# Last rows of w1 as 128 half rows on the main queue, hidden units numbered by halves, w1 issued first, small vectors on the second queue

## The chip, the cores and the metric

The kernel runs on one core of a Trainium2 chip. The core has five engines with instruction streams of their own: TensorE (PE, with its weight loads shown as PEld), VectorE (DVE), ScalarE (ACT), GpSimd (POOL) and SyncE (SP). SP and ACT also issue transfers between the chip's memory and the core's 128-partition memory; in the profile their issuing rows are SPq and ACTq, and their two queues are q1 and q10. The metric is the device time of one execution in microseconds, lower is better. The profile gives one execution in detail.

## The reference

Two branches of one decoder step are mixed by a gate. Eight tokens (B = 8), width D = 448.

```python
def _A_ref(x, k_cache, v_cache, wq, wo):      # 16 heads of 256 over 8 K/V heads, window W = 1024
    q = (x @ wq).reshape(B, Sq, Hq, Dh).transpose(0, 2, 1, 3)
    k = jnp.repeat(k_cache[:, :, Sk - W:, :], rep, axis=1)
    v = jnp.repeat(v_cache[:, :, Sk - W:, :], rep, axis=1)
    p = softmax(jnp.einsum("bhqd,bhkd->bhqk", q, k) * (Dh ** -0.5))
    o = jnp.einsum("bhqk,bhkd->bhqd", p, v)
    return o.transpose(0, 2, 1, 3).reshape(B, Sq, Hq * Dh) @ wo

def _B_ref(x, w1, b1, w2, b2):                # 448 -> 1792 -> 448
    h = gelu(jnp.einsum("bsd,df->bsf", layernorm(x), w1) + b1)
    return jnp.einsum("bsf,fd->bsd", h, w2) + b2

g = sigmoid((x * gate_w).sum(-1, keepdims=True))
return g * _A_ref(...) + (1 - g) * _B_ref(x, ...)
```

All inputs and the output are bfloat16. In bytes the K and V windows are nearly all: 64 pairs of token and K/V head, with one K tile and one V tile of 512 KB each.

## The kernel before

**Loads.** Nearly all transfers are issued by SP, in a fixed order: x (L121), the first 384 rows of w1 (L125), w2 (L130), three pieces of wq (L134) and wq's last 64 rows as 128 half rows (L135), then K tiles, V tiles and slices of wo in the order of the list `units`. ACT issues the gate vector (L122), the last 64 rows of w1 (L128) into partitions 0 to 63 of `w1_t`, b1 into partition 64 of the same tile (L129) and b2 (L131). K and V tiles share a ring of 23 buffers (NKV). A new tile is issued when the tile that had its buffer has been read, and each issue also waits for the transfer eight places earlier in the order of all issues of both queues; the order is written out by hand.

A row of w1 is one of D input features, a column one of F = 1792 hidden units. The first 384 features lie three to a partition in `w1_sb`. The last 64 features lie one to a partition in `w1_t`, with b1 below them as a 65th row; the transposed input `yT` has a row of ones there (the memset at L173).

**Start.** VectorE forms the gate's sum and the layer norm of x (L179 to L198), with a square root and a tanh on ScalarE. `transposed` (L207) turns y (three thirds and the last 64 columns) and x (three thirds and two spread halves `x_e`) into columns with TensorE and copies them out of PSUM.

**Feed-forward.** `mlp_up` (L231) works on 14 groups of 128 hidden units; unit q * 14 + k is unit q of group k. A group is four matmuls into eight columns of one PSUM tile: three for `w1_sb`, one of 65 partitions for `w1_t` and the bias. The gelu follows on VectorE and ScalarE, and `mlp_down` (L258) multiplies group by group with `w2_sb`, which holds 14 consecutive rows of w2 on each partition, in one run of 12544 bytes.

**Queries and attention.** Then q is formed from wq (L280 to L299), and the main loop (L432) runs over 64 pairs: `transposes` of a K tile, `scores` of the pair before, the softmax once per K/V head, and `pv` with the V tile of the pair eleven places back. `issue_to(NKV + done)` at the end of each step issues the next tiles on SP. After the loop comes the last projection and the gated sum (L458).

Of the kernel before, what the change touches and what calls it, by code (L numbers as in the profile page):

```python
# [11 lines left out]
BF16 = mybir.dt.bfloat16  # L12
# [4 lines left out]
def kernel(  # L17
# [15 lines left out]
    nc = tc.nc  # L33
    P = nc.NUM_PARTITIONS

    B, Sq, D = A_x.shape
# [4 lines left out]
    W = min(4096, max(256, Sk // 4))  # L41
    kv0 = Sk - W
    F = B_w1.shape[1]
    NB = B
    NJ = Dh // P
    NC = W // P
    NF = F // P
    R = NB * rep
    DC = D // P
    DM = DC * P  # L50
    TL = D - DM
    HH = HD // 2
    assert Sq == 1 and Dh % P == 0 and W % P == 0 and F % P == 0
    assert TL * 2 == P and TL % 32 == 0 and NC * R <= P and 3 * 32 <= P and R <= 32
    qscale = float(Dh) ** -0.5
    NPAIR = NB * Hkv
    LAG = 3
# [8 lines left out]
    xf = A_x.rearrange("b s d -> (b s) d")  # L66
    out_f = out.rearrange("b s d -> (b s) d")

    consts = ctx.enter_context(tc.tile_pool(name="consts", bufs=1))
# [3 lines left out]
    ps_kt = ctx.enter_context(  # L73
        tc.tile_pool(name="ps_kt", bufs=4, space=bass.MemoryType.PSUM)
    )
# [10 lines left out]
    x_sb = consts.tile([NB, D], BF16, name="x_sb")  # L86
# [1 line left out]
    wq_sb = consts.tile([P, DC, HD], BF16, name="wq_sb")  # L88
    wq_t = consts.tile([P, HH], BF16, name="wq_t")
    w1_sb = consts.tile([P, DC, F], BF16, name="w1_sb")  # L90
    w1_t = consts.tile([P, F], BF16, name="w1_t")
    w2_sb = consts.tile([P, NF, D], BF16, name="w2_sb")
    b2_sb = consts.tile([1, D], BF16, name="b2_sb")
    NKH = rep * NJ
    wo_sb = [consts.tile([P, NKH, D], BF16, name=f"wo_sb{g}") for g in range(Hkv)]
    ident = consts.tile([P, P], BF16, name="ident")
    identf = consts.tile([P, P], F32, name="identf")
    onesb = consts.tile([P, P], BF16, name="onesb")
    diag = [consts.tile([P, R], BF16, name=f"diag{k}") for k in range(2)]
    qT = consts.tile([P, NJ, Hkv, NB, rep], BF16, name="qT")  # L100
    xT = consts.tile([P, DC + 2, NB], BF16, name="xT")
    yT = consts.tile([P, DC + 1, NB], BF16, name="yT")
    x_e = consts.tile([NB, 2, P], BF16, name="x_e")
    g_sb = consts.tile([NB, 1], F32, name="g_sb")
    omg_sb = consts.tile([NB, 1], F32, name="omg_sb")
    bvec = consts.tile([NB, D], F32, name="bvec")
# [9 lines left out]
    def load(kind, n):  # L116
# [1 line left out]
        nc.sync.dma_start(t[:], k_src(A_k_cache if kind == "K" else A_v_cache, n))  # L118
        KV[kind, n] = t

    nc.sync.dma_start(x_sb[:], xf)  # L121
    nc.scalar.dma_start(  # L122
        gw_sb[:], gate_w.rearrange("(o d) -> o d", o=1).to_broadcast([NB, D])
    )
    nc.sync.dma_start(  # L125
        w1_sb[:], B_w1[0:DM, :].rearrange("(p c) n -> p c n", c=DC)
    )
    nc.scalar.dma_start(w1_t[0:TL, :], B_w1[DM:D, :])  # L128
    nc.scalar.dma_start(w1_t[TL : TL + 1, :], B_b1.rearrange("(o f) -> o f", o=1))  # L129
    nc.sync.dma_start(w2_sb[:], B_w2.rearrange("(p k) n -> p k n", k=NF))  # L130
    nc.scalar.dma_start(b2_sb[:], B_b2.rearrange("(o d) -> o d", o=1))  # L131
    wq_v = A_wq[0:DM, :].rearrange("(p c) n -> p c n", c=DC)
    for c in range(DC):
        nc.sync.dma_start(wq_sb[:, c, :], wq_v[:, c, :])  # L134
# [34 lines left out]
    for t in diag:  # L169
        nc.gpsimd.memset(t[:], 0.0)  # L170
    nc.gpsimd.memset(x_e[:], 0.0)
    nc.gpsimd.tensor_copy(identf[:], ident[:])
    nc.vector.memset(yT[:], 1.0)  # L173


    prod = consts.tile([NB, D], F32, name="prod")
# [9 lines left out]
    y_sb = consts.tile([NB, D], BF16, name="y_sb")  # L186
# [12 lines left out]

    A_ps = ps_a.tile([NB, D], F32, name="A_ps")  # L200

    for h in range(2):
        nc.vector.tensor_copy(
            x_e[:, h, :].rearrange("b (r h) -> b r h", h=2)[:, :, h], x_sb[:, DM:D]
        )

    def transposed(dst, parts):  # L207
        tp = ps_kt.tile([P, W], BF16, tag="ktp", name="tp")
        for c, s in enumerate(parts):
            w = s.shape[1]  # L210
            nc.tensor.transpose(  # L211
                tp[0:w, c * NB : (c + 1) * NB], s, ident[0:NB, 0:NB]
            )
        w = parts[-1].shape[1]
        full = len(parts) if w == P else len(parts) - 1
        v = tp[:, 0 : len(parts) * NB].rearrange("p (c b) -> p c b", b=NB)
        nc.vector.tensor_copy(dst[:, 0:full, :], v[:, 0:full, :])
        if w < P:
            nc.vector.tensor_copy(dst[0:w, full, :], v[0:w, full, :])

    def thirds(t):
        v = t[:, 0:DM].rearrange("b (p c) -> b c p", c=DC)
        return [v[:, c, :] for c in range(DC)]

    transposed(yT, thirds(y_sb) + [y_sb[:, DM:D]])
    transposed(xT, thirds(x_sb) + [x_e[:, h, :] for h in range(2)])


    M = {}

    def mlp_up():  # L231
        h_ps = ps_g.tile([P, 512], F32, tag="grp", name="h_ps")
        for k in range(NF):
            o = h_ps[:, k * NB : (k + 1) * NB]
            for c in range(DC + 1):
                w, kp = (w1_sb[:, c, :], P) if c < DC else (w1_t[0 : TL + 1, :], TL + 1)
                nc.tensor.matmul(  # L237
                    o,
                    lhsT=w.rearrange("p (q k) -> p k q", k=NF)[:, k, :],
                    rhs=yT[0:kp, c, :],  # L240
                    start=(c == 0),
                    stop=(c == DC),
                )
        N = NF * NB
        z = consts.tile([P, N], F32, name="z")
        u = consts.tile([P, N], F32, name="u")
        th = consts.tile([P, N], F32, name="th")
        hT = consts.tile([P, N], BF16, name="hT")
        nc.vector.tensor_copy(z[:], h_ps[:, 0:N])  # L249
        nc.vector.tensor_tensor(u[:], z[:], z[:], op=ALU.mult)  # L250
        nc.vector.tensor_scalar(u[:], u[:], 0.044715, 1.0, op0=ALU.mult, op1=ALU.add)
        nc.vector.tensor_tensor(u[:], u[:], z[:], op=ALU.mult)
        nc.scalar.activation(th[:], u[:], ACT.Tanh, scale=0.7978845608028654)
        nc.vector.tensor_scalar(th[:], th[:], 1.0, 0.5, op0=ALU.add, op1=ALU.mult)
        nc.vector.tensor_tensor(hT[:], th[:], z[:], op=ALU.mult)  # L255
        M["hT"] = hT

    def mlp_down():  # L258
# [13 lines left out]
        nc.vector.tensor_scalar_mul(bvec[:], b_ps[0:NB, 0:D], omg_sb[:])  # L272

    mlp_up()
    mlp_down()

# [3 lines left out]
    for c in range(DC + 1):  # L280
        for k in range(NQ):
            if c < DC:
                w, xs = wq_sb[:, c, k * P : (k + 1) * P], xT[:, c, :]
            else:
                h, kk = divmod(k, NQ // 2)
                w, xs = wq_t[:, kk * P : (kk + 1) * P], xT[:, DC + h, :]
            nc.tensor.matmul(
                q_ps[:, k * NB : (k + 1) * NB],
                lhsT=w,
                rhs=xs,  # L290
                start=(c == 0 and k == 0),
                stop=(c == DC),
# [139 lines left out]
    for n in range(LAST):  # L432
# [5 lines left out]
        g, r = divmod(n, NB)  # L438
# [53 lines left out]
```

## Time and profile before

| | |
|---|---|
| time, median of 3 runs | 202.74 us (202.69 to 202.88) |
| profiled execution, its own time | 202.94 us |
| its span | 201.2 us |
| granted TensorE clock, mean | 0.79 |
| PE / DVE busy | 161.7 / 106.7 us |
| moved by transfers | 78.15 MB, mean 389 GB/s |
| last V tile landed | 194.88 us |

How it is read: the times of a row count from the start of the span. Row 2 of the page cuts the span into 40 equal slices (5.03 us each) and gives the busy share of an engine in tenths, the busy share of the transfer engines, and GB/s. The chain that ended last is followed backwards from the last instruction, at each step to what released it. A stretch row gives, for a window of the span, the busy time of each engine, then the granted clock, the share of the transfer engines and GB/s. In rows of the timeline the first number is the start, the second the duration, and the bracket tells how long the engine had been idle and what ended that.

### The profile page before, as it was taken

What the parts mean: (1) busy time and instruction counts of PE and PEld (TensorE: products, weight loads), DVE (VectorE), ACT (ScalarE), POOL (GpSimd) and SP (SyncE); (2) the same over time, 40 slices, a digit from 0 to 9 for tenths busy, and PEclk for the clock granted to TensorE, in tenths of its full rate; (3) what the DMA queues carried; (4) which work ended last, traced back from release to release, by engine and by line L of the source; (5) the groups of instructions that cost most, each with busy time, mean ns of one, the idle gap of its engine ahead of it and who ended that gap; (6) DMA issues with size and microseconds to landing.
All of it is one profiled execution on the core that took longest, in us unless ns stands there. A gap on an engine that the chain in (4) does not pass through costs nothing.

```text
span 201.2 us, 7399 instructions
## 1 busy us (share of the span) xinstructions
PE 161.7 (80%) x3392; PEld 146.6 (73%) x3392; DVE 106.7 (53%) x241; ACT 5.6 (3%) x13; POOL 1.4 (1%) x11
## 2 busy tenths in 40 slices
PE   0268999987899759979898789777999899785753
PEld 0162799977898759879887789677897898785440
DVE  4220189995575526755495448544673658554001
ACT  3200000000000000000000000000000000000000
POOL 2000000000000000000000000000000000000000
PEclk9999979999669856985599757988556969975555
DMA  5999999999999999999999999999999999999930
GB/s 185 343 415 414 415 416 411 414 415 406 414 419 419 404 418 420 416 407 415 420 415 411 411 420 412 416 414 413 415 425 404 412 416 421 415 415 415 371 133 1
DMA packets 23682, 78.15 MB, mean 389 GB/s; under 512 B 2314, under 2 KB 6435, under 8 KB 23012
## 3 DMA queue, kind: packets, MB, share of 16 engines
q1 hardware_dynamic: 23552, 77.45, 95.9%
q8 instruction: 26, 0.43, 0.8%
q10 hardware_dynamic: 100, 0.24, 0.4%
q14 instruction: 4, 0.03, 0.0%
HBM read 77.68 MB, written 0.01 MB: 386 GB/s over the span
## 4 chain that ended last, share of the span: by engine, by line
DMA 91%; PE 6%; DVE 1%; issue 0%; ACTq 0%; SPq 0%; DVEq 0%
DMA kv<-in_A_v_cache_dram 42%; DMA kv<-in_A_k_cache_dram 40%; DMA wq_t<-in_A_wq_dram 6%; DMA w_t<-in_B_w_dram 4%; PE ktp L314 3%; PE A_ps L421 1%; PE grp L396 1%; PE grp L330 1%; DVE res L458 0%; ACTq L122 0%; DVE rz L387 0%; PE grp L382 0%; DVE ot L407 0%; SPq L118 0%; DVEq L387 0%
## 5 line engine op out<-in xcount | busy, mean ns | idle before, releaser
L319 DVE COPY kt<-ktp 128x1024 bf16<-128x1024 bf16 x128 | 84.2, 688 | 56.5 <-PE ktp L314 56.0
L314 PE MATMUL ktp<-ident,kv 128*128 128x128 bf16 x1024 | 86.2, 252 | 12.6 <-DMA kv<-in_A_k_cache_dram 12.6
L314 PEld LDWEIGHTS <-kv 128*128 128x128 bf16 x1024 | 74.5, 115 | 18.0 <-DMA kv<-in_A_k_cache_dram 16.1
L396 PE MATMUL grp<-e,kv 128*128 128x2 bf16 x1024 | 35.9, 165 | 9.1 <-DMA kv<-in_A_v_cache_dram 7.9
L396 PEld LDWEIGHTS <-kv 128*128 128x128 bf16 x1024 | 32.1, 100 | 13.0 <-DMA kv<-in_A_v_cache_dram 10.4
L330 PE MATMUL grp<-qT,kt 128*128 128x2 bf16 x1024 | 36.3, 165 | 0.3 <-DVE kt L319 0.2
L330 PEld LDWEIGHTS <-kt 128*128 128x128 bf16 x1024 | 34.8, 100 | 0.5 <-DVE kt L319 0.3
L421 PE MATMUL A_ps<-wo_sb,ot 128*8 128x448 bf16 x32 | 9.6, 433 | 0.6 <-DVE ot L407 0.6
L387 DVE RECIPROCAL rz<-grp 128x16 f32<-128x16 f32 x8 | 2.0, 254 | 11.6 <-PE grp L382 11.6
L261 PE MATMUL b_ps<-w_sb,hT 128*8 128x448 bf16 x14 | 5.4, 573 | 2.1 <-DVE hT L255 2.1
L377 ACT ACTIVATE e<-grp 128x128 bf16<-128x128 f32 x8 | 2.2, 278 | 167.3 <-PE grp L370 167.3
L261 PEld LDWEIGHTS <-hT 128*8 128x8 bf16 x14 | 1.6, 122 | 5.2 <-issue 2.9
L421 PEld LDWEIGHTS <-ot 128*8 128x8 bf16 x32 | 2.4, 93 | 3.4 <-issue 1.5
L211 PE MATMUL tp<-ident,y_sb 8*128 8x8 bf16 (+1 forms) x4 | 0.4, 181 | 5.5 <-DVE y_sb L193 5.5
L237 PE MATMUL h_ps<-yT,w_t 65*128 65x8 bf16 x14 | 2.8, 201 | 2.4 <-DMA w_t<-in_B_b_dram 2.4
L211 PEld LDWEIGHTS <-y_sb 8*128 8x128 bf16 (+1 forms) x4 | 0.3, 110 | 5.5 <-DVE y_sb L193 5.5
L237 PE MATMUL h_ps<-yT,w_sb 128*128 128x8 bf16 x42 | 3.5, 202 | 0.7 <-DMA w_sb<-in_B_w_dram 0.7
L237 PEld LDWEIGHTS <-w_sb 128*128 128x128 bf16 x42 | 3.4, 159 | 0.8 <-DMA w_sb<-in_B_w_dram 0.8
L237 PEld LDWEIGHTS <-w_t 65*128 65x128 bf16 x14 | 2.2, 158 | 2.4 <-DMA w_t<-in_B_w_dram 2.4
L249 DVE COPY z<-h_ps 128x112 f32<-128x112 f32 x1 | 0.3, 275 | 6.6 <-PE h_ps L237 6.6
L272 DVE TENSOR_SCALAR bvec<-b_ps,omg_sb 8x448 f32<-8x448 f32 x1 | 0.7, 672 | 5.7 <-PE b_ps L268 5.7
L370 PE MATMUL grp<-diag,onesb 128*128 128x128 bf16 x8 | 1.8, 229 | 2.3 <-DVE diag L364 2.0
(61 smaller groups left out, 44.6 us busy)
## 6 DMA issues: line engine op xcount, KB each, us to landing
kv<-in_A_k_cache_dram SPq DMA_DIRECT2D x64, 512.0 KB, 9.9
kv<-in_A_v_cache_dram SPq DMA_DIRECT2D x64, 512.0 KB, 9.9
wo_sb<-in_A_wo_dram SPq DMA_DIRECT2D x8, 448.0 KB, 9.9
wq_sb<-in_A_wq_dram SPq DMA_DIRECT2D x3, 1024.0 KB, 12.7
w_sb<-in_B_w_dram SPq DMA_DIRECT2D x1, 1568.0 KB, 10.7
w_sb<-in_B_w_dram SPq DMA_DIRECT2D x1, 1344.0 KB
wq_t<-in_A_wq_dram SPq DMA_DIRECT2D x1, 512.0 KB, 11.1
w_t<-in_B_w_dram ACTq DMA_DIRECT2D x1, 224.0 KB, 8.5
```

What stands on the lines that cost most here:

```text
L211: nc.tensor.transpose(tp[0:w, c * NB : (c + 1) * NB], s, ident[0:NB, 0:NB])
L237: nc.tensor.matmul(o, lhsT=w.rearrange("p (q k) -> p k q", k=NF)[:, k, :], rhs=yT[0:kp, c, :], start=(c == 0), stop=(c == DC),)
L261: nc.tensor.matmul(b_ps[0:NB, 0:D], lhsT=M["hT"][:, k * NB : (k + 1) * NB], rhs=w2_sb[:, k, :], start=(k == 0), stop=False,)
L272: nc.vector.tensor_scalar_mul(bvec[:], b_ps[0:NB, 0:D], omg_sb[:])
L314: nc.tensor.transpose(ktp[:, c * P : (c + 1) * P], K[:, c, j * P : (j + 1) * P], ident[:],)
L319: nc.vector.tensor_copy(kt[:, j, :], ktp[:])
L330: nc.tensor.matmul(G[g][:, s : s + rep], lhsT=kt[:, j, c * P : (c + 1) * P], rhs=qT[:, j, g, b, :], start=(b == 0 and c == 0 and j == 0), ...
L370: nc.tensor.matmul(G[g][:, S0 : S0 + NC * R].rearrange("p (c r) -> p c r", c=NC), lhsT=onesb[:], rhs=diag[g % 2][:].unsqueeze(1).to_broadc ...
L377: nc.scalar.activation(e[:], G[g][:, S0 : S0 + NC * R], ACT.Exp)
L387: nc.vector.reciprocal(rz[:], G[g][:, Z0 : Z0 + R])
L396: nc.tensor.matmul(G[g][:, o : o + rep], lhsT=V[:, c, j * P : (j + 1) * P], rhs=E[g][:, c * R + b * rep : c * R + (b + 1) * rep], start=False,
L421: nc.tensor.matmul(A_ps[:], lhsT=ot[:].rearrange("p j (b i) -> p j i b", i=rep)[:, j, i, :], rhs=w, start=(g == 0 and k == 0), stop=(g == ...
```

## The change

- SP's first issue is w1's first 384 rows. x is issued on ACT, with the gate vector, b1 and b2 behind it.
- The last 64 rows of w1 are issued on SP, behind w1's first rows, as 128 half rows: partition 2r + h holds half h of row r, 1792 bytes each. `w1_t` has half the columns. b1 has a tile of its own, `b1_sb`, with one partition.
- Because a partition now holds one half of the hidden units, these are numbered by halves: group k of half h. The input for the half rows is spread like `x_e` already was: `y_e` holds y's last 64 columns in every second place, zeros in the others, once for each half. `yT` gets a fifth block for it.
- A group is now five matmuls: three for `w1_sb`, one for the bias with a row of ones, one of 128 partitions for `w1_t`.
- w2 is laid out to match: each partition takes 7 consecutive rows from the first half of w2 and 7 from the second, two runs of 6272 bytes.
- The memset of `yT` and its second copy go; a memset of `y_e` on GpSimd and two copies into it on VectorE come.

```diff
@@ -51,7 +51,9 @@
     TL = D - DM
     HH = HD // 2
     assert Sq == 1 and Dh % P == 0 and W % P == 0 and F % P == 0
-    assert TL * 2 == P and TL % 32 == 0 and NC * R <= P and 3 * 32 <= P and R <= 32
+    FH = F // 2
+    NH = NF // 2
+    assert TL * 2 == P and NC * R <= P and 3 * 32 <= P and R <= 32 and NF % 2 == 0
     qscale = float(Dh) ** -0.5
     NPAIR = NB * Hkv
     LAG = 3
@@ -88,7 +90,8 @@
     wq_sb = consts.tile([P, DC, HD], BF16, name="wq_sb")
     wq_t = consts.tile([P, HH], BF16, name="wq_t")
     w1_sb = consts.tile([P, DC, F], BF16, name="w1_sb")
-    w1_t = consts.tile([P, F], BF16, name="w1_t")
+    w1_t = consts.tile([P, FH], BF16, name="w1_t")
+    b1_sb = consts.tile([1, F], BF16, name="b1_sb")
     w2_sb = consts.tile([P, NF, D], BF16, name="w2_sb")
     b2_sb = consts.tile([1, D], BF16, name="b2_sb")
     NKH = rep * NJ
@@ -99,8 +102,9 @@
     diag = [consts.tile([P, R], BF16, name=f"diag{k}") for k in range(2)]
     qT = consts.tile([P, NJ, Hkv, NB, rep], BF16, name="qT")
     xT = consts.tile([P, DC + 2, NB], BF16, name="xT")
-    yT = consts.tile([P, DC + 1, NB], BF16, name="yT")
+    yT = consts.tile([P, DC + 2, NB], BF16, name="yT")
     x_e = consts.tile([NB, 2, P], BF16, name="x_e")
+    y_e = consts.tile([NB, 2, P], BF16, name="y_e")
     g_sb = consts.tile([NB, 1], F32, name="g_sb")
     omg_sb = consts.tile([NB, 1], F32, name="omg_sb")
     bvec = consts.tile([NB, D], F32, name="bvec")
@@ -118,17 +122,18 @@
         nc.sync.dma_start(t[:], k_src(A_k_cache if kind == "K" else A_v_cache, n))
         KV[kind, n] = t
 
-    nc.sync.dma_start(x_sb[:], xf)
+    nc.scalar.dma_start(x_sb[:], xf)
     nc.scalar.dma_start(
         gw_sb[:], gate_w.rearrange("(o d) -> o d", o=1).to_broadcast([NB, D])
     )
+    nc.scalar.dma_start(b1_sb[:], B_b1.rearrange("(o f) -> o f", o=1))
+    nc.scalar.dma_start(b2_sb[:], B_b2.rearrange("(o d) -> o d", o=1))
     nc.sync.dma_start(
         w1_sb[:], B_w1[0:DM, :].rearrange("(p c) n -> p c n", c=DC)
     )
-    nc.scalar.dma_start(w1_t[0:TL, :], B_w1[DM:D, :])
-    nc.scalar.dma_start(w1_t[TL : TL + 1, :], B_b1.rearrange("(o f) -> o f", o=1))
-    nc.sync.dma_start(w2_sb[:], B_w2.rearrange("(p k) n -> p k n", k=NF))
-    nc.scalar.dma_start(b2_sb[:], B_b2.rearrange("(o d) -> o d", o=1))
+    nc.sync.dma_start(w1_t[:], B_w1[DM:D, :].rearrange("r (h n) -> (r h) n", h=2))
+    w2_v = w2_sb[:].rearrange("p (h k) n -> p h k n", h=2)
+    nc.sync.dma_start(w2_v, B_w2.rearrange("(h p k) n -> p h k n", h=2, k=NH))
     wq_v = A_wq[0:DM, :].rearrange("(p c) n -> p c n", c=DC)
     for c in range(DC):
         nc.sync.dma_start(wq_sb[:, c, :], wq_v[:, c, :])
@@ -169,8 +174,8 @@
     for t in diag:
         nc.gpsimd.memset(t[:], 0.0)
     nc.gpsimd.memset(x_e[:], 0.0)
+    nc.gpsimd.memset(y_e[:], 0.0)
     nc.gpsimd.tensor_copy(identf[:], ident[:])
-    nc.vector.memset(yT[:], 1.0)
 
 
     prod = consts.tile([NB, D], F32, name="prod")
@@ -199,47 +204,54 @@
 
     A_ps = ps_a.tile([NB, D], F32, name="A_ps")
 
-    for h in range(2):
+    def halves(dst, src):
+        for h in range(2):
+            nc.vector.tensor_copy(
+                dst[:, h, :].rearrange("b (r h) -> b r h", h=2)[:, :, h],
+                src[:, DM:D],
+            )
+
+    def transposed(dst, t, t_e):
+        v = t[:, 0:DM].rearrange("b (p c) -> b c p", c=DC)
+        parts = [v[:, c, :] for c in range(DC)] + [t_e[:, h, :] for h in range(2)]
+        tp = ps_kt.tile([P, W], BF16, tag="ktp", name="tp")
+        for c, part in enumerate(parts):
+            nc.tensor.transpose(
+                tp[:, c * NB : (c + 1) * NB], part, ident[0:NB, 0:NB]
+            )
         nc.vector.tensor_copy(
-            x_e[:, h, :].rearrange("b (r h) -> b r h", h=2)[:, :, h], x_sb[:, DM:D]
+            dst[:], tp[:, 0 : len(parts) * NB].rearrange("p (c b) -> p c b", b=NB)
         )
 
-    def transposed(dst, parts):
-        tp = ps_kt.tile([P, W], BF16, tag="ktp", name="tp")
-        for c, s in enumerate(parts):
-            w = s.shape[1]
-            nc.tensor.transpose(
-                tp[0:w, c * NB : (c + 1) * NB], s, ident[0:NB, 0:NB]
-            )
-        w = parts[-1].shape[1]
-        full = len(parts) if w == P else len(parts) - 1
-        v = tp[:, 0 : len(parts) * NB].rearrange("p (c b) -> p c b", b=NB)
-        nc.vector.tensor_copy(dst[:, 0:full, :], v[:, 0:full, :])
-        if w < P:
-            nc.vector.tensor_copy(dst[0:w, full, :], v[0:w, full, :])
-
-    def thirds(t):
-        v = t[:, 0:DM].rearrange("b (p c) -> b c p", c=DC)
-        return [v[:, c, :] for c in range(DC)]
-
-    transposed(yT, thirds(y_sb) + [y_sb[:, DM:D]])
-    transposed(xT, thirds(x_sb) + [x_e[:, h, :] for h in range(2)])
+    halves(y_e, y_sb)
+    transposed(yT, y_sb, y_e)
+    halves(x_e, x_sb)
+    transposed(xT, x_sb, x_e)
 
 
     M = {}
 
     def mlp_up():
         h_ps = ps_g.tile([P, 512], F32, tag="grp", name="h_ps")
-        for k in range(NF):
-            o = h_ps[:, k * NB : (k + 1) * NB]
-            for c in range(DC + 1):
-                w, kp = (w1_sb[:, c, :], P) if c < DC else (w1_t[0 : TL + 1, :], TL + 1)
+        for h in range(2):
+            for k in range(NH):
+                o = h_ps[:, (h * NH + k) * NB : (h * NH + k + 1) * NB]
+
+                def cols(w):
+                    return w.rearrange("p (q k) -> p k q", k=NH)[:, k, :]
+
+                for c in range(DC):
+                    nc.tensor.matmul(
+                        o, lhsT=cols(w1_sb[:, c, h * FH : (h + 1) * FH]),
+                        rhs=yT[:, c, :], start=(c == 0), stop=False,
+                    )
                 nc.tensor.matmul(
-                    o,
-                    lhsT=w.rearrange("p (q k) -> p k q", k=NF)[:, k, :],
-                    rhs=yT[0:kp, c, :],
-                    start=(c == 0),
-                    stop=(c == DC),
+                    o, lhsT=cols(b1_sb[:, h * FH : (h + 1) * FH]),
+                    rhs=onesb[0:1, 0:NB], start=False, stop=False,
+                )
+                nc.tensor.matmul(
+                    o, lhsT=cols(w1_t[:]), rhs=yT[:, DC + h, :],
+                    start=False, stop=True,
                 )
         N = NF * NB
         z = consts.tile([P, N], F32, name="z")
```

## The prediction

> **What bounds the kernel now.** I read the page from the coarse to the fine: the busy shares, the 40 slices, the chain that ended last, then stretches of the start, and last the queue waits.
>
> ```profile
> PE 161.7 (80%) x3392; PEld 146.6 (73%) x3392; DVE 106.7 (53%) x241; ACT 5.6 (3%) x13; POOL 1.4 (1%) x11
> DMA  5999999999999999999999999999999999999930
> GB/s 185 343 415 414 415 416 411 414 415 406 414 419 419 404 418 420 416 407 415 420 415 411 411 420 412 416 414 413 415 425 404 412 416 421 415 415 415 371 133 1
> q1 hardware_dynamic: 23552, 77.45, 95.9%
> q10 hardware_dynamic: 100, 0.24, 0.4%
> DMA 91%; PE 6%; DVE 1%; issue 0%; ACTq 0%; SPq 0%; DVEq 0%
> ```
>
> TensorE is busy 80% of the span, but the transfers take 91% of the chain, and from the third slice almost to the end the core moves about 415 GB/s without a pause. So 78.15 MB at a fixed pace set the time: a transfer that starts or ends earlier in the first 12 us moves everything behind it, and compute counts only where it would stop the transfers. Below the pace are only slices 1 and 2 (185 and 343) and the tail. The edit lies in those two slices, so I cut them finer (the last column is GB/s):
>
> ```profile
> 2.00:4.00 2.00, 0.00 (x0) 0.00 (x0) 1.50 (x4) 1.27 (x1) 0.02 (x1) 1.00 0.87 247
> 4.00:6.50 2.50, 0.56 (x7) 0.44 (x7) 1.11 (x5) 1.79 (x4) 0.00 (x0) 1.00 0.99 404
> 6.50:10.50 4.00, 0.63 (x5) 0.46 (x5) 0.67 (x6) 0.00 (x0) 0.00 (x0) 1.00 1.03 334
> 10.50:12.00 1.50, 1.46 (x25) 1.49 (x26) 0.00 (x0) 0.00 (x0) 0.00 (x0) 1.00 0.92 387
> 12.00:20.00 8.00, 5.87 (x42) 3.14 (x42) 1.54 (x6) 0.30 (x1) 0.00 (x0) 1.00 1.01 418
> ```
>
> The stream of weights starts slowly, reaches 404, falls back to 334 between 6.5 and 10.5 us, and recovers. The DMA share stays near 1 meanwhile: the engines hold packets, and the packets are slow. What is special there? The queue rows and the waits of the start say it:
>
> ```profile
> 0.74 0.37 SPq L121 DMA_DIRECT2D x_sb<-in_A_x_dram  x1
> 1.16 0.36 SPq L125 DMA_DIRECT2D w_sb<-in_B_w_dram  x1
> 1.35 0.52 ACTq L128 DMA_DIRECT2D w_t<-in_B_w_dram  x1
> 1.35 8.52 DMA w_t<-in_B_w_dram
> 10.54 0.20 PE L237 MATMUL h_ps<-yT,w_t 65*128 65x8 bf16 x1 [2.36 <-DMA w_t<-in_B_b_dram]
> 52.32 1.89 PE L314 MATMUL ktp<-ident,kv 128*128 128x128 bf16 x16 [0.66 <-DMA kv<-in_A_k_cache_dram]
> ```
>
> The 64 rows of w1 on ACT's queue take from 1.35 to 9.87. In the trace's packets they run only from 6.0 to 9.0 us, beside the last of w1 and the first of w2; in that time a 12544-byte packet of w2 takes up to 0.91 us, and 0.475 us once they are through. The last row shows when TensorE has worked off its late start: at 52.3 us it waits for a K tile for the first time.
>
> **The change part by part.** The sum is made against the profiled execution: span 201.2 us, its own time 202.94, so 1.7 us lie around it. It stands 0.20 above the median of the runs, 202.74; I subtract the gain from the median.
>
> *w1 first on SP.* One issue (x, 0.37 us, and the gap to the next row) leaves SP ahead of w1, so w1 is issued at 0.74 in place of 1.16. The packets of x came 1.17 us after their issue, those of w1 1.22 us, so the packets follow the issue: gain 0.42. It could be nothing if the slow ramp (247 GB/s from 2 to 4 us) belonged to the chip's first microseconds and not to w1; the rows that show no such thing are x and the gate vector, whose 896-byte packets already ran in about 0.04 us at 1.9 to 2.2. I take 0.42; ends 0 and 0.47.
>
> *w1's last rows from ACT's queue to SP's, from 64 partitions to 128.* The bytes stay. What goes is the mixture between 4 and 12 us. Against the steady 415, the stretches lost 2.5 x 11/415 = 0.07, 4 x 81/415 = 0.78 and 1.5 x 28/415 = 0.10, together 0.95 us. In the new form the rows go like the half rows of wq (L135, already 128 of them on SP), in whose stretch (12 to 20) the pace is 418. I take 0.90 of the 0.95, since the last stretch may hold something else; ends 0 and 0.99 (the loss by single packets against 423).
>
> The 64 rows are the only transfer of size that reaches half the partitions. [...]
>
> *w2 as two half rows per partition.* 128 packets of 12544 bytes become 256 of 6272, and w1's tail 128 of 1792 for 64 of 3584: 192 more, 12 for each of 16 engines. The nearest small packets are wo's 896-byte ones: the stretch 30.5 to 31.5 moves 390 GB/s, 32 to 33 moves 416, so 448 KB in 512 packets cost 1.18 in place of 1.10 us, 2.3 ns for each of an engine's 32. Twelve such are 0.03 us: taken. Ends: 0, and all of w2 and w1's tail at 390, which is 1.83 MB x (1/390 - 1/415), 0.28 us. Their order on SP (w1, w1's tail, w2) costs one more issue, about 0.35 us, while w1's 1344 KB run for 4 us: nothing.
>
> *SP's issue waits.* SP waits with each issue for an earlier transfer, counted over both queues in eights. Before, the second wq piece waits for a small vector, and wq_t for w1's rows until 9.87. Now the second wq piece waits for x, the third for w1, wq_t for the gate vector, the first K tile for b1. Worst case: x's few packets get behind w1's, as w1's rows did (issued 1.35, first packet 6.0), and land near 7. Until then w1, its tail, w2 and one wq piece (4.26 MB, 10 us at 415) are issued, enough until about 12. The same holds for b1, which landed at about 10.4 before: at that time all of wq is queued, until about 19. Cost 0, cover 5 us and more.
>
> *Vector work and TensorE.* The gate vector is now second on ACT, one issue (0.6 us) later than 0.74, and VectorE's first product waits for it and x, with the statistics behind it. If it too gets behind w1, it lands near 7 in place of 2.46. From that product to the first matmul of the layer took 2.46 to 7.12, and two copies into y_e (0.29), a wait for the gate's tanh and the transposes add about 0.5: the layer begins near 12 in place of 10.5. The 14 bias matmuls add 14 x 0.06 = 0.84 us (the 56 of the layer now run from 10.5 to 13.85, 0.06 each). So the first K transpose could come at about 27 in place of 24.8, or 1 us early if the vectors are not held up. What covers it: 23 buffers; the 24th tile is issued at 44.91, and the buffer that it takes was read by 26.7. The cover is 18 us, the delay under 3: cost 0. In the other direction nothing is won, since TensorE waits for tiles from 52 us on. The memset of yT that goes (0.09), the one of y_e on POOL (about 0.3 at 1.8 us, read after 5) and the one copy in place of two into yT lie in the same cover.
>
> Sum: 0.42 + 0.90 - 0.03 = 1.29 us. 202.94 becomes 201.65, the median 202.74 becomes 201.45.
>
> **The rivals.**
>
> *A: the dip is w2's own.* For it: the packets of w1's rows beside w1, from 6.0 to 6.45, ran at full pace (0.14 us each), the slow ones begin with w2's first packet, and w2's packets still take 0.58 at 9.2, when the rows are through. Against it: w1 and wq reach full pace at once after their first packets, and w2 is the same kind of read. Then only the start remains: 202.74 - 0.42 + 0.03 = 202.35, on the edge of no change. [...]
>
> *B: the start is not w1's to win.* The ramp stays where it is in time: 202.74 - 0.90 + 0.03 = 201.87. For it speaks that half of w1's first packets took over 0.9 us.
>
> *C, slower: w2 in halves is read slowly.* If the slow pace comes from how w2 is laid out, two streams 0.8 MB apart may keep it for all of w2. Price: the worst whole microsecond, 7 to 8, moves (108 + 383)/2 = 246 GB/s; 1.606 MB take 6.53 us there, 3.87 at 415, so 2.66 lost, and 202.74 - 1.29 + 2.66 = 204.1. It decides from the pace at which w2 loses 1.29: 1.606 MB in 5.16 us, 311 GB/s. Against it: wo's rows of 896 bytes, scattered more finely, keep 390.
>
> **How the numbers follow.** The main case has 0.57, A 0.19, B 0.12, C 0.07; 0.05 is left for a tail or a stream that behaves otherwise, both ways. Below 0.2%, 0.41 us here, this kernel's measurement can't tell a change. Main and B are faster, C slower, A almost on the bound, 202.33, taken as one part faster and three parts the same. Faster 0.75, same 0.16, slower 0.09. The range reaches down to both gains at their upper ends (0.47 + 0.99, so 201.28) with 0.13 for the spread of runs, and up over B to just past A: 201.15 to 202.45.
>
> **What would show it.** Right: w1's issue at 0.74 and its stream 0.4 us earlier; no stretch under 390 GB/s between 4 and 12 us; w2's packets (6272 bytes) near 0.24 us from the first; every later slice at 415; the last V tile near 193.6 in place of 194.9, and the tail behind it as long as before (6.3 us). TensorE's first K transpose may come anywhere from 23.5 to 27.5. Wrong: a dip at the same place with no second queue in it (A), or through all of w2 (C); the first full-pace microsecond still at 4 (B); a slice below 400 after 12 us, which would mean that the vectors' or TensorE's lateness reached the transfers after all.

## The result and the profile after

The changed kernel takes 205.52 us (205.44 to 205.69) against 202.80 before: 1.0138 times, 95% interval 1.0126 to 1.015. The forecast was 201.45, faster. The profiled execution has a span of 203.9 us and a time of 205.69.

Five lines of the page after, in the order of the page: the busy shares, the rate in 40 slices, the main queue, the chain that ended last, the landing time of a K tile.

```profile
PE 167.9 (82%) x3407; PEld 150.1 (74%) x3407; DVE 107.5 (53%) x241; ACT 5.6 (3%) x13; POOL 1.7 (1%) x12
GB/s 219 417 432 413 408 401 405 407 404 402 407 407 405 403 407 405 406 400 409 407 406 402 405 409 402 404 403 410 407 404 406 406 405 406 411 406 406 352 117 1
q1 hardware_dynamic: 23808, 77.68, 96.1%
DMA 48%; PE 38%; DVE 9%; issue 3%; ACT 1%; ACTq 0%; SPq 0%; DVEq 0%
kv<-in_A_k_cache_dram SPq DMA_DIRECT2D x64, 512.0 KB, 10.2
```

The start did what was forecast: slices 1 to 3 move 219, 417 and 432 GB/s where they moved 185, 343 and 415. The loss is in slices 4 to 37: 400 to 413 in place of 404 to 425. They are the same bytes, there in the same order, a little slower all the way. The stretches (the last column is GB/s) say where it begins:

```profile
4.00:6.50 2.50, 0.00 (x0) 0.00 (x0) 0.00 (x0) 0.00 (x0) 0.00 (x0) 1.00 0.95 384
6.50:10.50 4.00, 0.24 (x3) 0.15 (x3) 2.47 (x7) 1.77 (x3) 0.00 (x0) 1.00 1.03 426
12.00:20.00 8.00, 6.37 (x70) 5.82 (x70) 1.31 (x6) 0.30 (x1) 0.00 (x0) 1.00 1.01 421
20.00:40.00 20.00, 19.50 (x357) 15.51 (x358) 10.47 (x19) 0.00 (x0) 0.00 (x0) 0.91 1.03 406
40.00:180.00 140.00, 128.12 (x2708) 119.06 (x2704) 87.48 (x188) 1.94 (x7) 0.00 (x0) 0.76 1.03 405
```

The last two of the kernel before:

```profile
20.00:40.00 20.00, 19.91 (x453) 18.57 (x452) 14.67 (x26) 0.00 (x0) 0.00 (x0) 0.91 1.03 414
40.00:180.00 140.00, 121.50 (x2617) 114.05 (x2615) 82.78 (x180) 1.95 (x7) 0.00 (x0) 0.79 1.03 415
```

The dip of 334 GB/s is gone. The row from 4.00 to 6.50, 384, lies under the 390 that the prediction's sign allowed; it counts a packet's bytes where the packet starts, and with the bytes spread over each packet's time it is 412. The last of wq's three large pieces is out at 18.0 us in place of 19.3, 1.3 us earlier, as the sum had it. From 20 us on the pace is 405 in place of 415. In the trace's packets the 4096-byte ones, which are the K and V tiles and, 128 of 16512, wq's last rows, took 159.9 ns on average before and 163.2 after; before 0.8% of them took over 160 ns, after 66%.

What differs from 20 us on? Not the order, not the sources. The built programs show one difference that reaches all K and V transfers: where the tiles lie in the core's memory. The constants' pool stands ahead of the K and V ring, and it grew by 2336 bytes per partition: `w1_t` lost 1792, `b1_sb` added 3584, `y_e` 512, and the fifth block of `yT` 16, rounded up to 32. So the K and V buffers moved from byte 112896, which is 441 x 256, to 115232, which is 450 x 256 + 32. That was theory 1. The chain of waits offered theory 2: its TensorE share rose from 6 to 38%, since the vectors got behind w1's packets and the first K transpose came at 29.41 us in place of 24.80. Five rows of the chain after:

```profile
1.35 5.21 DMA gw_sb<-in_gate_w_dram
6.66 0.62 DVE prod L184
9.01 1.28 ACT L197
20.50 5.39 PE b_ps L273 x14
26.27 3.29 PE q_ps L299 x128
```

Theory 3 was that the new order of the first transfers leaves the 16 transfer engines in a phase that lasts.

### The profile page after: what moved, and what is told of

Its sections match the earlier page's. It is cut to its first block, busy times and chain, and to the rows that moved or that the text cites. A ratio compares the mean times of both kernels' runs of the same rounds, so it can differ in the third digit from the quotient of the medians.

```text
span 203.9 us, 7429 instructions
## 1 busy us (share of the span) xinstructions
PE 167.9 (82%) x3407; PEld 150.1 (74%) x3407; DVE 107.5 (53%) x241; ACT 5.6 (3%) x13; POOL 1.7 (1%) x12
## 4 chain that ended last, share of the span: by engine, by line
DMA 48%; PE 38%; DVE 9%; issue 3%; ACT 1%; ACTq 0%; SPq 0%; DVEq 0%
DMA kv<-in_A_v_cache_dram 26%; PE ktp L326 17%; DMA kv<-in_A_k_cache_dram 15%; DVE kt L331 5%; DMA wo_sb<-in_A_wo_dram 5%; PE grp L342 5%; PE grp L408 5%; PE A_ps L433 3%; PE b_ps L273 3%; DMA gw_sb<-in_gate_w_dram 3%; PE q_ps L299 2%; PE h_ps L244 1%; PE h_ps L252 1%; PE h_ps L248 1%; ACT L197 1%
## 5 line engine op out<-in xcount | busy, mean ns | idle before, releaser
L326 PE MATMUL ktp<-ident,kv 128*128 128x128 bf16 x1024 | 87.9, 255 | 8.9 <-DMA kv<-in_A_k_cache_dram 6.7
L326 PEld LDWEIGHTS <-kv 128*128 128x128 bf16 x1024 | 75.8, 116 | 15.4 <-DMA kv<-in_A_k_cache_dram 9.2
L408 PEld LDWEIGHTS <-kv 128*128 128x128 bf16 x1024 | 32.1, 100 | 10.1 <-DMA kv<-in_A_v_cache_dram 8.7
L433 PE MATMUL A_ps<-wo_sb,ot 128*8 128x448 bf16 x32 | 12.5, 540 | 0.6 <-DVE ot L419 0.6
L244 PE MATMUL h_ps<-yT,w_sb 128*128 128x8 bf16 x42 | 4.2, 195 | 0.0
L184 DVE TENSOR_TENSOR prod<-x_sb,gw_sb 8x448 f32<-8x448 bf16 x1 | 0.6, 614 | 6.7 <-DMA gw_sb<-in_gate_w_dram 6.7
L252 PE MATMUL h_ps<-yT,w_t 128*128 128x8 bf16 x14 | 3.0, 214 | 0.0
```

The costliest lines, as they stand in the source:

```text
L244: nc.tensor.matmul(o, lhsT=cols(w1_sb[:, c, h * FH : (h + 1) * FH]), rhs=yT[:, c, :], start=(c == 0), stop=False,)
L252: nc.tensor.matmul(o, lhsT=cols(w1_t[:]), rhs=yT[:, DC + h, :], start=False, stop=True,)
L326: nc.tensor.transpose(ktp[:, c * P : (c + 1) * P], K[:, c, j * P : (j + 1) * P], ident[:],)
L408: nc.tensor.matmul(G[g][:, o : o + rep], lhsT=V[:, c, j * P : (j + 1) * P], rhs=E[g][:, c * R + b * rep : c * R + (b + 1) * rep], start=False,
L433: nc.tensor.matmul(A_ps[:], lhsT=ot[:].rearrange("p j (b i) -> p j i b", i=rep)[:, j, i, :], rhs=w, start=(g == 0 and k == 0), stop=(g == ...
```

## The experiments

### Where the 2.7 us come from

Four kernels, run beside the kernel before (203.02 us in this group). Each ratio below is against the kernel before as it ran in the same group. An unused tile at the end of the constants moves the ring and the small tiles around it, and leaves the order and size of all transfers as they are.

```diff
     res = consts.tile([NB, D], BF16, name="res")
+    pad = consts.tile([P, 112], BF16, name="pad")    # changed kernel, 224 bytes
```

> The changed kernel with one unused tile of 224 bytes per partition behind `res`, which moves the K and V buffers (and what lies behind them) from 32 bytes past a multiple of 256 to a multiple of 256, where the kernel before had them. Theory 1, the place of the K and V buffers slows their packets (159 ns before, 163 after): packets back at 159 ns, stretch 40 to 180 back at 415 GB/s, time 201.4 us, 1.3 below the kernel before, since the start had gained that much. Theory 2, the 4.7 us later start of TensorE costs the time: nothing changes, 205.5. Theory 3, the new order of the first transfers leaves the engines in another phase for the whole stream: nothing changes, 205.5.

Measured: 201.38 us, 0.9919 of the kernel before (0.9904 to 0.9933). 224 unused bytes are worth 4.1 us, and bring the forecast time. The stretches of this run, 20 to 40 and 40 to 180 us, and its landing row:

```profile
20.00:40.00 20.00, 19.50 (x365) 15.79 (x366) 10.87 (x20) 0.00 (x0) 0.00 (x0) 0.91 1.03 415
40.00:180.00 140.00, 128.60 (x2746) 120.75 (x2744) 88.09 (x189) 1.95 (x7) 0.00 (x0) 0.76 1.03 415
kv<-in_A_k_cache_dram SPq DMA_DIRECT2D x64, 512.0 KB, 9.9
```

The packets are back at 159.8 ns, a K tile lands 0.3 us sooner, and TensorE still starts late (first K transpose at 29.16).

```diff
     res = consts.tile([NB, D], BF16, name="res")
+    pad = consts.tile([P, 16], BF16, name="pad")     # kernel before, 32 bytes
```

> The kernel before with one unused tile of 32 bytes per partition, nothing else: K and V buffers 32 bytes past a multiple of 256. Theory 1: packets at 163 ns, 405 GB/s from 40 to 180, 202.8 + 4.0 = 206.8 us. Theories 2 and 3: 202.8, since order and start are the old ones.

Measured: 207.04 us, 1.0196 (1.018 to 1.0211); packets 163.3 ns. The two stretches:

```profile
20.00:40.00 20.00, 19.84 (x455) 18.66 (x454) 14.78 (x27) 0.00 (x0) 0.00 (x0) 0.91 1.03 405
40.00:180.00 140.00, 125.03 (x2535) 115.92 (x2533) 81.41 (x176) 1.94 (x7) 0.00 (x0) 0.71 1.03 405
```

The old order, the old start and an early TensorE lose the same 10 GB/s once the ring stands 32 bytes off. Theories 2 and 3 have no way to explain this run.

```diff
     res = consts.tile([NB, D], BF16, name="res")
+    pad = consts.tile([P, 16], BF16, name="pad")     # changed kernel, 32 bytes
```

> The changed kernel with an unused tile of 32 bytes: K and V buffers 64 past a multiple of 256. Theory 1 with a step at 64 bytes: as with 224 bytes, 201.4 us. Theory 1 with a step at 128 or 256 bytes: 205.5, or in between. Theories 2 and 3: 205.5.

Measured: 205.44 us, 1.0118 (1.0101 to 1.0135), packets 163.3. 64 bytes past a multiple is as bad as 32.

```diff
-    nc.scalar.dma_start(x_sb[:], xf)
+    nc.sync.dma_start(x_sb[:], xf)          # changed kernel; the gate vector is then first on ACT
```

> The changed kernel with x issued first on SP again, and the gate vector first on ACT, so that both run ahead of w1; buffers stay 32 past a multiple of 256. The first K transpose should come near 24 us in place of 29.5. Theory 1: packets stay at 163 ns, time 205.5 to 206.0 (the later w1 costs up to 0.4). Theory 2: most of the 4 us comes back, 201.5 to 202. Theory 3: somewhere between, and the packets change.

Measured: 205.97 us, 1.0146 (1.0131 to 1.0162), packets 163.3, the first K transpose at 25.42. TensorE is 4 us earlier and the kernel 0.45 us slower than the changed kernel (205.52, in another group; 0.53 against the run 64 bytes off in this one). Theory 2 falls. The 0.45 fits w1's issue, which is 0.42 later again; the medians of the kernel before, 202.71 to 203.02 in the groups, show how rough such a small difference is.

Is it really the transfers' target, or something behind the ring that moved with it?

```diff
+    padpool = ctx.enter_context(tc.tile_pool(name="padpool", bufs=1))   # behind the ring
     ktpool = ctx.enter_context(tc.tile_pool(name="ktpool", bufs=3))
...
+    pad = padpool.tile([P, 16], BF16, name="pad")    # kernel before, 32 bytes
```

> The kernel before with the 32 unused bytes behind the K and V buffers: these stay on a multiple of 256, and only the transposed K tiles (kt) and the softmax's small tiles move by 32. If the place of the transfers' targets is what counts: 202.7, packets 159 ns. If the place of what TensorE and VectorE read and write counts: up to 207.0, as with the 32 bytes ahead of the buffers.

Measured: 202.77 us, 0.9995 (0.9985 to 1.0004), packets 159.9. Moving the transposed K tiles and the softmax's tiles changes nothing; only the K and V buffers count. These are written by the transfers and read by TensorE, and the reading is not needed: from 20 to 29 us, before TensorE's first K transpose, the 4096-byte packets already took 163.2 ns in the changed kernel, and 159.5 with 224 bytes.

Which step? The changed kernel with 96 and with 480 bytes in the same place, in two runs:

```diff
     res = consts.tile([NB, D], BF16, name="res")
+    pad = consts.tile([P, 48], BF16, name="pad")     # 96 bytes
...
+    pad = consts.tile([P, 240], BF16, name="pad")    # in the other run: 480 bytes
```

> The changed kernel with 96 unused bytes: K and V buffers 128 past a multiple of 256. Measured so far: 32 past, 163 ns and 205.5 us; 64 past, the same, 205.4; on a multiple, 159 ns and 201.4. If only a multiple of 256 is good: 205.4. If 128 is enough: 201.4.

> The changed kernel with 480 unused bytes: K and V buffers on a multiple of 512 in place of 256. If 256 is the step: 201.4, packets 159 ns. If a larger step helps further: packets below 159 ns and a time below 201.2.

Measured: 205.28 us (1.0125, 1.0108 to 1.0142) with the ring 128 past a multiple of 256, packets 163.2; 201.41 us (0.9922, 0.9908 to 0.9937) on a multiple of 512, packets 159.9. So 32, 64 and 128 past a multiple of 256 cost the same 4 us, a multiple of 256 is enough, and one of 512 brings no more.

```diff
     gw_sb = consts.tile([NB, D], BF16, name="gw_sb")
+    pad0 = consts.tile([P, 64], BF16, name="pad0")    # 128 bytes ahead of wq, w1, w2
...
     b2_sb = consts.tile([1, D], BF16, name="b2_sb")
+    pad1 = consts.tile([P, 64], BF16, name="pad1")    # 128 ahead of wo
...
     res = consts.tile([NB, D], BF16, name="res")
+    pad2 = consts.tile([P, 112], BF16, name="pad2")   # 224 ahead of the ring
```

> As with 480 unused bytes, but 128 of them ahead of wq and 128 ahead of wo, so that wq, w1, w2 and wo too lie on multiples of 256 (they are 128 past one otherwise, wo excepted). If each packet off a multiple pays about 4 ns whatever its size: wq's 8192-byte packets fall from 309 to 305 ns, w1's and w2's likewise, together 48 of them on each engine, 0.2 us less than with 480 bytes behind everything. If only packets of 4096 bytes pay: no difference, 201.4.

Measured: 201.33 us, 0.992 (0.9903 to 0.9937), wq's packets 309 ns with and without. These packets of 8192 bytes paid nothing for a place 128 past a multiple, so the cost is not a fixed sum on each packet, whatever its size.

### What the start was worth

The dip between 6.5 and 10.5 us had three possible causes: two queues side by side, half the partitions, or w2 itself. The kernel before was run beside these (202.71 us).

```diff
-    nc.scalar.dma_start(w1_t[0:TL, :], B_w1[DM:D, :])
+    nc.sync.dma_start(w1_t[0:TL, :], B_w1[DM:D, :])      # kernel before
```

> The kernel before with its 64 rows of w1 issued on SP, behind w1's first rows, instead of on ACT; x still first, all places in memory as before (so K and V packets at 159 ns). What makes the slow stretch from 6.5 to 10.5 us (0.95 us lost)? If two queues side by side: the dip goes, 202.9 - 0.95 = 201.95. If the 64 partitions: the dip stays, between 202.4 (half of it, as the rows now run in one block) and 202.9. If w2 itself: the dip stays at w2's first packets, 202.9.

Measured: 202.51 us, 0.9993 (0.9984 to 1.0003): no difference that can be told. The dip stays, shorter. Two stretches of the kernel before, then the same two of this run:

```profile
6.50:8.50 2.00, 0.63 (x5) 0.46 (x5) 0.67 (x6) 0.00 (x0) 0.00 (x0) 1.00 1.03 272
8.50:10.50 2.00, 0.00 (x0) 0.00 (x0) 0.00 (x0) 0.00 (x0) 0.00 (x0) 1.00 1.03 397
6.50:8.50 2.00, 0.68 (x6) 0.54 (x7) 0.75 (x7) 0.00 (x0) 0.00 (x0) 1.00 1.09 339
8.50:10.50 2.00, 2.00 (x35) 2.00 (x36) 0.00 (x0) 0.00 (x0) 0.00 (x0) 1.00 0.99 420
```

By its packets the loss is 0.57 us against a pace of 423 (half microseconds from 6.0 to 8.5 at 421, 315, 223, 267 and 411, with the bytes of a packet spread over its time); before it was 0.99 counted in the same way. So one queue instead of two spares about 0.4 us of the dip; of that the time shows at most 0.2, within its interval.

```diff
-    nc.scalar.dma_start(w1_t[0:TL, :], B_w1[DM:D, :])
+    nc.gpsimd.memset(w1_t[0:TL, :], 0.0)                 # kernel before
```

> The kernel before without the transfer of the 64 rows of w1 (zeros are written there, so the last 64 features are left out of the feed-forward). 224 KB less is 0.55 us at 415 GB/s. If the dip is w2's own: it stays, 202.9 - 0.55 = 202.35. If it belongs to the 64 rows, by queue or by partitions: 202.9 - 0.55 - 0.95 = 201.4, and w2's packets take 0.475 us from the first.

Measured: 201.17 us, 0.9923 (0.9908 to 0.9938), 1.54 us less, of which 0.55 are the bytes; the other 0.99 is the size of the dip. w2's packets take 469 ns from the first on:

```profile
6.50:8.50 2.00, 1.45 (x23) 1.44 (x23) 0.81 (x7) 0.03 (x1) 0.00 (x0) 1.00 0.95 408
8.50:10.50 2.00, 2.00 (x37) 2.00 (x36) 0.00 (x0) 0.00 (x0) 0.00 (x0) 1.00 1.01 428
```

The dip is not w2's own. It comes and goes with the 64 rows.

```diff
-    nc.sync.dma_start(w1_t[:], B_w1[DM:D, :].rearrange("r (h n) -> (r h) n", h=2))
+    nc.scalar.dma_start(w1_t[:], B_w1[DM:D, :].rearrange("r (h n) -> (r h) n", h=2))   # ahead of b1; with 224 bytes
```

> The changed kernel with the 224 unused bytes (201.4 us), and the 128 half rows of w1 issued on ACT, behind x and the gate vector, instead of on SP. If two queues side by side make the dip: it comes back, 201.4 + 0.95 = 202.35. If the 64 partitions do: no dip, 201.4. If w2's single long runs do: no dip either, 201.4.

Measured: 201.38 us, 0.9936 (0.992 to 0.9952), the same median as with the half rows on SP (in another group), and no dip although both queues run side by side:

```profile
6.50:8.50 2.00, 0.00 (x0) 0.00 (x0) 1.66 (x4) 0.00 (x0) 0.00 (x0) 1.00 1.04 425
8.50:10.50 2.00, 0.24 (x3) 0.15 (x3) 0.81 (x4) 1.62 (x3) 0.00 (x0) 1.00 1.02 428
```

So a second queue alone makes no dip: beside 128 partitions it costs nothing, beside the 64 rows it makes the dip longer, 0.99 us in place of 0.57. What is left is the 64 partitions. This run also has w2 in 6272-byte packets, and no run puts 128 half rows beside w2's 12544-byte packets, so that the long packets take part is not excluded. For the partitions speaks that, in the kernel before with its rows on SP, the rows' own packets go from 140 ns to 200 and more from 6.63 us on, when a single packet of w2 had begun. How 64 partitions come to slow them no run shows.

Last, the start without w1 at its head, in the changed kernel with 224 bytes (202.80 us for the kernel before in this group):

```diff
-    nc.scalar.dma_start(x_sb[:], xf)
+    nc.sync.dma_start(x_sb[:], xf)
```

> The changed kernel with the 224 unused bytes and x and the gate vector ahead of w1 again: TensorE's first K transpose near 25.4 us in place of 29.2, w1 0.4 us later. If TensorE's late start costs nothing and w1's order is worth its issue: 201.4 + 0.45 = 201.85. If the late start costs something once the packets are fast: below 201.4.

Measured: 201.77 us, 0.9942 (0.9927 to 0.9957); first K transpose at 24.31 in place of 29.16. Against the two changed kernels beside it on a multiple of 512 (201.41 and 201.33) that is 0.36 to 0.44 slower, which is what w1's issue, 0.42 later, would give. So five microseconds of TensorE's lateness cost nothing that can be seen, and w1's place at the head is worth about 0.4.

## Why the prediction was wrong

**The step that failed** is "from the third slice almost to the end the core moves about 415 GB/s without a pause", taken as a fixed pace that the change only shifts: "a transfer that starts or ends earlier in the first 12 us moves everything behind it". The pace was not fixed. The sum listed what the new tiles hold and when they land, but had no term for where they push the tiles behind them. Measured, this term is 205.52 - 201.38 = 4.1 us, and 4.1 and 4.0 in the pairs within one group (205.44 - 201.38, 207.04 - 203.02). From the packets: 16512 of 4096 bytes are 1032 for each of 16 engines, times 163.2 - 159.8 = 3.4 ns, is 3.5 us. What else ran beside them was slowed too: the 26 packets of 16384 bytes on the instruction queue (q8) took 1078 ns in place of 932 with 224 bytes, some 0.2 us for each engine if they are spread evenly. The other 0.4 was not traced to its place. Why a packet off the step takes longer stays open.

None of the rivals had it either. Rival C came out on the right side for another reason and is refuted: w2's 6272-byte packets took 243 ns on average in the changed kernel, and the stretch from 6.5 to 10.5 us moved 426 GB/s. The sign in the profile that the prediction named, a slice below 400 after 12 us, was set too coarse: a stream that loses 2.4% in every slice stayed at 400 to 413. Two of its signs of being right did fail in plain sight: the later slices stand near 405, not 415, and the last V tile landed at 197.63, not near 193.6 (193.35 with 224 bytes).

**What the start was to bring held.** w1 first: 0.42 forecast, its first packet came at 1.78 in place of 2.14, and x put first again cost 0.36 to 0.53. The rows of w1 on all partitions: 0.90 taken of 0.95; with x ahead of w1 as before and the ring on its step, 202.80 - 201.77 = 1.03 measured, for this and all else that the change does. The extra packets: 0.03, too small to be seen; the changed kernel's start is free of dips. In all 1.29 forecast, and measured with the ring on its old step, each against the kernel before in its own group, 202.80 - 201.41 = 1.39 and 203.02 - 201.38 = 1.64. Rival A falls with the run without the 64 rows, where w2 runs at full pace from its first packet, and B with w1's earlier packets. One reading was off without harm: the packet times of the prediction are 0.24 us late on the span's clock (x's first packet is at 1.67, that of w1's rows at 5.77), and the sum uses only differences.

**TensorE's lateness** was costed at nothing, with 18 us of cover, and cost nothing; but its size was wrong. The gate vector did wait behind w1 (it ended the idle time at 6.66), and the layer began at 11.9 as worked out. The first layer then took 6.5 us, not the 4.2 of 70 matmuls at 0.06: a group of five takes 0.45, where a group of four took 0.24 before; why is not shown. So the K transposes began at 29.41, not 27. The chain after counts all this as its own, 38% TensorE, and is no help here. With 224 bytes the share is larger still, in a kernel 4.1 us faster:

```profile
PE 45%; DMA 39%; DVE 11%; issue 3%; ACT 1%; ACTq 0%; SPq 0%; DVEq 0%
```

The chain follows who released whom, and a late engine that is catching up releases buffers just as a limiting one does.

**Could it have been seen?** Yes, in the built program, not in the profile before: the ring's first byte stood at 112896 and moved to 115232. The trace before shows one place only, so the price could not be read from it. The runs show a step of 256 for the K and V buffers, with packets 2.1% longer at each of 32, 64 and 128 bytes past it, and none for wq's 8192-byte packets, at 309 ns 128 off and on the step.

## What to carry to other kernels

When a change adds or resizes any tile, compare the addresses of every buffer behind it that takes part in the limiting stream, before working out anything else; here a ring 32 bytes off cost three times what the change had gained. A transfer-bound kernel is worth a look at whether its ring starts on a multiple of 256 bytes, which was worth 4.1 us here, and a pad costs one line. The transfer that reached only 64 partitions slowed its neighbours here: w2's 12544-byte packets took up to 912 ns in the kernel before, 469 in the run without the 64 rows. Spreading it over 128, with what came along, was worth 1.03 us, where its bytes alone take 0.55.

The best version measured is the changed kernel with the pad: 201.38 us with 224 bytes, 201.33 with all large tiles on the step, which can't be told apart.

## What the runs showed that I had not expected

- 4096-byte packets into K and V buffers off a 256-byte step take 163.2 to 163.3 ns on average in place of 159.8 to 159.9, whether 32, 64 or 128 off. That is 4 us on 201.
- Place does not cost every packet. wq's last rows, also in 4096-byte packets and 128 off, took 159.2 to 159.8 ns in the changed kernel with its ring 32, 64 or 128 off, and wq's 8192-byte packets, 128 off, showed nothing over 8 us. The first K tile, from 18.8 us on, took 159.4, 162.2 and 161.7 ns with the ring 32, 64 and 128 off, and the tiles behind it about 163 in all three. What sets the K and V tiles apart is open; that the cost builds up as such packets follow one another is possible and was not tested.
- A vector of 896-byte rows issued 0.6 us behind a 1.3 MB transfer on the other queue landed 5.2 us after its issue; issued ahead of it, within 1.8 us. It cost no time that can be seen here; the prediction had worked out 18 us of cover for it.
